# Gate and value products of the second chunk in whole float32, with the first chunks' due dates made anew

## The chip, the cores and the metric

The kernel runs on one core of one Trainium2 chip. The metric is the time of one execution on the device, in microseconds. Lower is better. A core has five engines that run side by side, each with its own queue, taken in order: TensorE (PE), which multiplies matrices; VectorE (DVE), ScalarE (ACT) and GpSimd (POOL), which work element by element; and SyncE (SP), which here issues every transfer between main memory and the core. They wait for each other by semaphores.

## The reference

The inputs are q, k and v of 8 batches, 8 heads, 576 tokens and 64 elements a head, and the weights of a channel mix of width 512 with 1024 hidden elements.

```python
k_p = k.reshape(B, H, Sp, pool, D).mean(axis=3)      # pool = 8: 72 pooled keys
v_p = v.reshape(B, H, Sp, pool, D).mean(axis=3)
scores = scale * np.matmul(q, k_p.transpose(0, 1, 3, 2))
attn = softmax(scores)                               # maximum taken off, 1e-9 added to the sum
x = np.matmul(attn, v_p)                             # heads side by side: 512 wide
x_prev = x shifted by one token, zero at a batch's start
xk = mu_k * x + (1.0 - mu_k) * x_prev
xr = mu_r * x + (1.0 - mu_r) * x_prev
k = np.maximum(xk @ w_k, 0.0)
v = k * k @ w_v
r = 1.0 / (1.0 + np.exp(-(xr @ w_r)))
out = r * v
```

## The kernel before

The 4608 tokens of all batches are one row of 13 chunks: 128, 256 and eleven times 384 tokens. A tile is 128 tokens. Each chunk goes through the same steps, and each step is a generator function that issues instructions and names what it needs:

- `softmax`, `part`, `transposed`, `transposed_rest` (one tile): scores on PE, maximum, exponential and sum on DVE and ACT, normalised on DVE or POOL, turned on PE. `BY_HEAD` lists the tiles whose exponentials are taken head by head on ACT, with the maximum as a bias and the sum taken along, in place of two passes on DVE.
- `attended` (one quarter of the width, c and g): probabilities times pooled values on PE; `shifted` and `joined` make the two mixes with the previous token, for keys (xk) and gates (xr).
- `hidden` (c, jt: 8 per chunk): the key products, xk times w_k, then the square of their positive part.
- `gate` (c, tt: one per tile): xr times w_r, and a sigmoid. `mixed` (c, tt): the squares times w_v, times the gate, and out.

**Whole and split.** A product of two float32 operands can be made in two ways here. Whole: one float32 matmul. Split: each operand x is stored as a high half h (a cast to the format float32r) and a low half l = x - h, and three float32r matmuls h*h + l*h + h*l are added. A split operand costs a cast on ACT and a subtraction on DVE or POOL: `x_parts` for the mixes (names xkh, xkl, xrh, xrl), the end of `hidden` for the squares (sh, sl), `split` for the weights (w_k, w_r, w_v from got_wk, got_wr, got_wv). Before the change, only chunk 0 is whole (`WHOLE`) and its attention and that of chunk 1 (`WHOLE_ATT`). The weights arrive as 64-bit words, and `convert` makes float32 of them (L528 on ACT, L530 and L533 on DVE). `split` (L555 on ACT, L558 on DVE or POOL by `LOW_BY`) waits until the whole products that read the full weight are done, and each split waits for the one before it, since its two halves take a buffer that the one before gave back.

**What sets the order.** The kernel builds its instruction streams before it runs: `Order.run` keeps all steps as threads, with a due date each, estimates when each engine is free, and takes the step that is ready with the earliest due date. `EARLIER` is a table that is added to the due dates by name (softmax 3, hidden 1 4, split v 2); a step that is not in it keeps its plain date. The order that comes out is fixed in the program: on the chip an engine runs its list in turn, and an instruction that waits holds up all that stand behind it. `LOADS` is the order of the first transfers on SP's queue: k, v, r and q followed by a number are keys, values, the last pooled values and queries; wk, wr and wv are the weights; c are constants. Keys and values land in staging buffers, of which few exist, so a load can wait until the sums over its predecessor are done. Two tiles under early_sl and one under early_xrl are extra landing places: they lie in the buffers that chunk 1 or 2 later use for sl and xrl. `SUM_BY` names the engine of a pooling sum (t is PE, v DVE, g POOL).

At the start PE runs `warm` (L430) and 40 fillers (L440), matmuls whose results nobody reads.

## Time and profile before

| | |
|---|---|
| runs shown | 641.62, 641.49 and 643.84 us; median 641.62 |
| profiled execution | 642.56 us, span 640.8 us |
| granted TensorE clock | 1.0 throughout |
| first matmul of chunk 0's key products | 28.91 us from the span's start |
| first matmul of chunk 2's key products | 104.58 us |
| busy over the span | PE 622.0, DVE 410.1, ACT 358.6, POOL 216.7 us |
| transfers | 50.48 MB, mean 79 GB/s |

The page gives busy time by engine, the span in slices, the transfer queues, the chain of work that ended last, the costliest groups of instructions, and the transfers. Times in the trace are from the start of the span. A line such as L1082 is a line of the kernel before. In a group of instructions, the names are out<-in with buffer numbers left out, then partitions x elements, the count, the busy time, the mean duration of one in ns, and the idle time of the engine just before them with what ended it. A whole float32 matmul is recorded as two matmuls. The records of matmuls that follow each other overlap, so the step from one to the next is read from a run of them, not from the mean of one.

### The profile page before, as it was taken

To read this page: it belongs to the slowest core of one execution; us is meant where nothing else is said; L and a number is where in the kernel's file an instruction comes from. 1 tells how busy PE (TensorE), PEld (TensorE's weight loads), DVE (VectorE), ACT (ScalarE), POOL (GpSimd) and SP (SyncE) were. 2 spreads that over 40 slices of the span, in tenths; PEclk is the share of its full clock that TensorE was granted. 3 is DMA by queue.
4 is the path that set the end of the run, shared out by engine and by line. 5 is a ranking of instruction groups with operands and counts; after the bars stand their busy time and mean duration, and the time that the engine had idled before them with its cause. 6 is when DMAs were issued, how large, how long until landed. Compare 5 with 4: busy or idle time off the path is not lost.

```text
span 640.8 us, 9433 instructions
## 1 busy us (share of the span) xinstructions
PE 622.0 (97%) x3411; PEld 552.0 (86%) x3411; DVE 410.1 (64%) x803; ACT 358.6 (56%) x788; POOL 216.7 (34%) x342
## 2 busy tenths in 40 slices
...
GB/s 338 257 389 121 92 143 46 97 136 64 109 74 50 50 1 18 173 90 34 18 27 163 58 16 34 34 25 166 58 21 38 42 17 18 34 0 17 34 1 50
DMA packets 19007, 50.48 MB, mean 79 GB/s; under 512 B 2256, under 2 KB 2512, under 8 KB 18960
## 3 DMA queue, kind: packets, MB, share of 16 engines
...
## 4 chain that ended last, share of the span: by engine, by line
PE 78%; DVE 12%; ACT 4%; POOL 3%; DMA 2%; issue 1%; SPq 0%; DVEq 0%; POOLq 0%; ACTq 0%
PE mm L1034 27%; PE mm L1115 25%; PE mm L1082 15%; PE bank L937 4%; PE sc L735 4%; DVE xm L990 2%; PE bank L839 2%; POOL xkl L1008 1%; DVE sl L1058 1%; DMA got_wk<-in_w_k 1%; POOL xrl L1008 1%; PE bank L440 1%; ACT t L950 1%; DVE pr L876 1%; DVE stage L565 1%
## 5 line engine op out<-in xcount | busy, mean ns | idle before, releaser
L1034 PE MATMUL mm<-xkh,w_k 128*128 128x384 f32 (+1 forms) x768 | 194.3, 335 | 1.1 <-DVE rk L1050 1.1
L1115 PE MATMUL mm<-w_v,sh 128*128 128x512 f32 x560 | 186.7, 396 | 0.7 <-DVE w_v L558 0.7
L1034 PEld LDWEIGHTS mm<-xkh,w_k 128*128 128x128 f32 x768 | 136.2, 188 | 3.9 <-DVE rk L1050 2.2
L1034 PE MATMUL mm<-xkl,w_k 128*128 128x384 f32 (+1 forms) x384 | 126.9, 330 | 0.0
L1115 PEld LDWEIGHTS mm<-w_v,sh 128*128 128x128 f32 x560 | 105.4, 188 | 21.6 <-DVE w_v L558 1.2
L1115 PE MATMUL mm<-w_v,sl 128*128 128x512 f32 x280 | 109.3, 390 | 0.0
L1082 PE MATMUL mm<-w_r,xrh 128*128 128x512 f32 x280 | 90.8, 396 | 1.5 <-DVE rk L1050 1.5
L990 DVE SCALAR_TENSOR_TENSOR xm<-bank,given,t 128x384 f32<-128x384 f32 (+1 forms) x96 | 54.5, 601 | 44.9 <-POOL t L965 27.2
L1056 ACT CAST sh<-rk 128x384 fp32r<-128x384 f32 (+1 forms) x96 | 48.3, 505 | 57.9 <-DVE rk L1050 57.5
L1058 DVE TENSOR_TENSOR sl<-rk,sh 128x384 fp32r<-128x384 f32 (+1 forms) x96 | 57.1, 597 | 28.0 <-ACT sh L1056 27.4
L1008 POOL TENSOR_TENSOR xkl<-xm,xkh 128x384 fp32r<-128x384 f32 (+1 forms) x48 | 48.2, 1003 | 78.2 <-ACT xkh L1006 78.0
L1034 PEld LDWEIGHTS mm<-xkl,w_k 128*128 128x128 f32 x384 | 72.2, 188 | 0.1
L950 ACT ACTIVATE t<-bank,om_sb 128x384 f32<-128x384 f32 (+1 forms) x96 | 48.0, 570 | 39.2 <-PE bank L937 39.2
L797 POOL TENSOR_TENSOR px<-e,sm 128x64 f32<-128x64 f32 (+1 forms) x33 | 10.4, 314 | 160.3 <-DVE sm L791 150.5
L1043 ACT ACTIVATE rk<-mm 128x384 f32<-128x384 f32 (+1 forms) x96 | 46.0, 480 | 33.1 <-PE mm L1034 25.9
L1082 PEld LDWEIGHTS mm<-w_r,xrh 128*128 128x128 f32 x280 | 52.6, 188 | 12.7 <-DVE rk L1050 1.9
L1125 DVE TENSOR_TENSOR rs<-mm,rs 128x512 f32<-128x512 f32 x36 | 24.6, 684 | 60.3 <-PE mm L1115 60.1
L1050 DVE SCALAR_TENSOR_TENSOR rk<-mm,rk 128x384 f32<-128x384 f32 (+1 forms) x96 | 51.6, 540 | 17.9 <-ACT rk L1043 17.7
L1115 PEld LDWEIGHTS mm<-w_v,sl 128*128 128x128 f32 x280 | 52.8, 188 | 8.9
L1082 PE MATMUL mm<-w_r,xrl 128*128 128x512 f32 x140 | 54.6, 390 | 0.0
L565 POOL TENSOR_TENSOR stage<-stage 128x512 f32<-128x512 f32 (+5 forms) x57 | 48.6, 861 | 2.0
L1008 POOL TENSOR_TENSOR xrl<-xm,xrh 128x384 fp32r<-128x384 f32 (+1 forms) x48 | 48.1, 1002 | 2.5 <-ACT xrh L1006 2.4
...
## 6 DMA issues: line engine op xcount, KB each, us to landing
...
stage<-in_vm SPq DMA_DIRECT2D x15, 512.0 KB, 4.3
got_wk<-in_w_k SPq DMA_DIRECT2D x8, 512.0 KB, 6.9
got_wv<-in_w_v SPq DMA_DIRECT2D x8, 512.0 KB, 9.6
...
got_wr<-in_w_r SPq DMA_DIRECT2D x4, 512.0 KB, 8.9
```

Source lines behind the costliest of these rows:

```text
L565: nc_eng.tensor_tensor(out=st[:, :, :w], in0=st[:, :, :w], in1=st[:, :, w:2 * w], op=ALU.add)
L735: nc.tensor.matmul(out=halves[g // 2][o:o + n, 0, k:k + 2 * KEYS], lhsT=qs[:, g, o:o + n], rhs=kbd[b % 2][:, g, :], start=True, stop=True,)
L950: nc.scalar.activation(out=ts[m][:, 1:n + 1], in_=xp, func=AF.Copy, scale=om_sb[:, m, g:g + 1])
L990: nc.vector.scalar_tensor_tensor(out=xm[:, :n], in0=bank[:, :n], scalar=mu_sb[:, m, g:g + 1], in1=ts, op0=ALU.mult, op1=ALU.add,)
L1008: nc.gpsimd.tensor_tensor(out=lo, in0=xm[:, :n], in1=hi, op=ALU.subtract)
L1034: nc.tensor.matmul(out=hp, lhsT=w[:, o], rhs=x[:, ct, :n], start=(ct == 0 and k == 0), stop=(ct == NCT - 1 and k == len(terms) - 1),)
L1043: nc.scalar.activation(out=rk[:, :n], in_=hp, func=AF.Relu)
L1050: nc.vector.scalar_tensor_tensor(out=rk[:, :n], in0=hp, scalar=0.0, in1=rk[:, :n], op0=ALU.max, op1=ALU.mult)
L1056: nc.scalar.copy(out=sh[:, :n], in_=rk[:, :n])
L1058: nc.vector.tensor_tensor(out=operand("sl", c)[:, jt, :n], in0=rk[:, :n], in1=sh[:, :n], op=ALU.subtract)
L1082: nc.tensor.matmul(out=bank, lhsT=x[:, ct, o], rhs=w, start=(ct == 0 and k == 0), stop=(ct == NCT - 1 and k == len(terms) - 1),)
L1115: nc.tensor.matmul(out=bank, lhsT=s[:, o], rhs=w, start=(jt == 0 and k == 0), stop=(jt == NJT - 1 and k == len(terms) - 1),)
```

## The change

Chunk 1's gate products and value products become whole; its key products stay split. `WHOLE_GATE` and `WHOLE_MIX` name the chunks for which that holds. With it go `x_parts` of chunk 1's gate input, the cast and the low half of its squares, and its waits for the early tiles in sl and xrl, which it no longer uses. The splits of w_r and w_v now wait for chunk 1's products too. Tile 6 joins `BY_HEAD`. The transfers at the start stand in a new order, the table of due dates is new and ends with chunk 3, where it ended with chunk 4, and the planner counts 0.43 rather than 0.86 us for a warming matmul.

```diff
--- before.py
+++ after.py
@@ -33,6 +33,8 @@
 CH = max(CHUNKS)
 
 WHOLE = (0,)
+WHOLE_GATE = (0, 1)
+WHOLE_MIX = (0, 1)
 WHOLE_ATT = (0, 1)
 TWICE = 3
 PACKED = (0, 1)
@@ -43,76 +45,66 @@
 REBASE = 2.0 ** -((1023 - 127) // 8)
 
 LOADS = (
-    "k0 k1 k2 q0 r0 q1 c0 wk0 v0 k3 q2 wk1 wk2 wk3 wk4 v1 wk5 r1 q4 wk6 wk7 q3 v3 wr0 wr1 wr2 wr3 "
-    "wv0 wv1 wv2 q5 wv3 wv4 wv5 wv6 wv7 v2 "
+    "k0 c0 wk0 q0 k1 wk1 r0 wk2 q1 q2 v0 v1 k2 wk3 q4 wk4 r1 wk5 q3 k3 wk6 v3 wk7 q5 wr0 wr1 wr2 wr3 "
+    "wv0 wv1 wv2 v2 wv3 wv4 wv5 wv6 wv7 "
 )
 
 SUM_BY = {"k0": "t", "k1": "v", "v0": "t", "v1": "t", "r0": "t", "k2": "v", "k3": "v", "v2": "g", "v3": "v", "r1": "g"}
 
-NORM_BY = {0: 'g', 1: 'v', 2: 'v', 3: 'v', 4: 'g', 6: 'g', 5: 'v'}
+NORM_BY = {0: 'g', 1: 'v', 2: 'v', 3: 'v', 4: 'g', 6: 'g', 5: 'v', 7: 'g'}
 WARMING = 4
 FILLERS = 40
 
 LOW_BY = {"k": "gvgvvvgv", "r": "gvgv", "v": "gvvggvgv"}
-BY_HEAD = ((0, 1), (2, 0))
+BY_HEAD = ((0, 1), (2, 0), (6, 0))
 
 BESIDE = (1,)
 SQUARED_ON_ACT = (8, 0)
 COPIES_ON_ACT = ()
 
 EARLIER = {
-    "warm": 192.0, "constants": 417.1, "complements": 5357.6, "loads": 265.4, "keys 0 0": 155.5,
...
+    "filling": 484.5, "warm": 561.9, "constants": 6.9, "complements": 129.2, "loads": 322.9,
...
 }
 PLAN = ""
 SPARE = 0.5
@@ -313,7 +305,8 @@
         if c in WHOLE:
             return whole_operands[kind]
         if (kind, c) not in operands:
-            dtype = F32 if kind == "pth" and c in WHOLE_ATT else F32R
+            whole = {"pth": WHOLE_ATT, "xrh": WHOLE_GATE, "sh": WHOLE_MIX}.get(kind, ())
+            dtype = F32 if c in whole else F32R
             operands[kind, c] = sb.tile(shapes[kind], dtype, name=f"{kind}_{c}", tag=kind)
         return operands[kind, c]
 
@@ -327,7 +320,8 @@
         return every(kind, c - 1) if c > 1 else []
 
     def free_of_early(c, tag):
-        return [("early", t, i) for t, n in EARLY for i in range(n) if t == tag and c not in WHOLE]
+        kept = c in {"sl": WHOLE_MIX, "xrl": WHOLE_GATE}[tag]
+        return [("early", t, i) for t, n in EARLY for i in range(n) if t == tag and not kept]
 
     slots("rs", CH // P, [P, DM])
     slots("t", 2, [P, 2, CH + 1])
@@ -426,7 +420,7 @@
         nc.vector.memset(zeros, 0.0)
         bank = yield take("bank")
         for _ in range(WARMING):
-            yield "pe", 0.86, False
+            yield "pe", 0.43, False
             nc.tensor.matmul(out=bank[:, :256], lhsT=zeros[:, :P], rhs=zeros[:, :256], start=True, stop=True)
         order.give("bank", bank)
         order.give("tmp", zeros)
@@ -980,9 +974,10 @@
         n = CHUNKS[c]
         whole = c in WHOLE
         bank, t = held["t", c, g]
-        if whole:
+        direct = whole or m and c in WHOLE_GATE
+        if direct:
             xm = operand(f"x{'kr'[m]}h", c)[:, g]
-            ts = xm[:, :n]
+            ts = xm[:, :n] if whole else t[:, m, :n]
         else:
             xm = yield take("xm")
             ts = t[:, m, :n]
@@ -994,7 +989,7 @@
             if t is not None:
                 order.give("t", t)
             order.give("mm" if whole and g == NPAIR - 1 else "bank", bank)
-        if whole:
+        if direct:
             order.make(("x", c, g, m))
         else:
             order.add(att_due[c] + g, x_parts(c, g, m, xm))
@@ -1038,7 +1033,8 @@
         order.make(("hid", c, jt))
         yield need(*before("mixed", c), *free_of_early(c, "sl"))
         sh = operand("sh", c)[:, jt]
-        rk = sh if whole else (yield take("rk"))
+        kept = c in WHOLE_MIX
+        rk = sh if kept else (yield take("rk"))
         yield act(n)
         nc.scalar.activation(out=rk[:, :n], in_=hp, func=AF.Relu)
         if c < 2 and jt < SQUARED_ON_ACT[c]:
@@ -1051,7 +1047,7 @@
                 out=rk[:, :n], in0=hp, scalar=0.0, in1=rk[:, :n], op0=ALU.max, op1=ALU.mult
             )
             order.give("mm", bank)
-        if not whole:
+        if not kept:
             yield act(n)
             nc.scalar.copy(out=sh[:, :n], in_=rk[:, :n])
             yield dve(n)
@@ -1062,7 +1058,7 @@
         order.make(("s", c, jt))
 
     def gate(c, tt):
-        whole = c in WHOLE
+        whole = c in WHOLE_GATE
         last = tt == CHUNKS[c] // P - 1
         yield need(*([("gating", c, tt - 1)] if tt else every("hid", c)))
         bank = yield take("mm")
@@ -1084,7 +1080,7 @@
                     start=(ct == 0 and k == 0), stop=(ct == NCT - 1 and k == len(terms) - 1),
                 )
         order.make(("gated", c, tt))
-        if last and whole:
+        if last and c in WHOLE:
             order.give("stage", stage[1])
         yield act(DM, "sigmoid")
         nc.scalar.activation(out=rs, in_=bank, func=AF.Sigmoid)
@@ -1093,7 +1089,7 @@
         order.make(("gate", c, tt))
 
     def mixed(c, tt):
-        whole = c in WHOLE
+        whole = c in WHOLE_MIX
         last = tt == CHUNKS[c] // P - 1
         yield need(*every("gated", c))
         if tt:
@@ -1103,7 +1099,7 @@
         for jt in range(NJT):
             yield need(("s", c, jt), ("full" if whole else "parts", "v", jt))
             yield pe(DM, whole, 1 if whole else 3)
-            if jt == 0 and whole or jt == NJT - 1:
+            if jt == 0 and c in WHOLE or jt == NJT - 1:
                 order.make(("mixing", c, tt))
             if whole:
                 terms = [(operand("sh", c)[:, jt], full["v", jt])]
@@ -1117,7 +1113,7 @@
                     start=(jt == 0 and k == 0), stop=(jt == NJT - 1 and k == len(terms) - 1),
                 )
         order.make(("mixed", c, tt))
-        if last and whole:
+        if last and c in WHOLE:
             order.give("stage", stage[2])
         yield need(("gate", c, tt))
         rs = held.pop(("rs", c, tt))
@@ -1149,7 +1145,8 @@
             at = {"k": FIRST + 2.6 * i - 4, "r": FIRST + 20 + 2 * i - 3, "v": FIRST + 28 + 2.5 * i}[kind]
             order.add(at, convert(kind, i))
             used = [("hid", c, i) for c in WHOLE] if kind == "k" else [
-                k for c in WHOLE for k in every({"r": "gated", "v": "mixed"}[kind], c)
+                k for c in {"r": WHOLE_GATE, "v": WHOLE_MIX}[kind]
+                for k in every({"r": "gated", "v": "mixed"}[kind], c)
             ]
             at = {"k": 2.1 * i - 4, "r": 15 + i, "v": 25 + 0.8 * i}[kind]
             order.add(later + at, split(kind, i, *used))
```

Three places show how the change moves instructions. Lines of the changed kernel stand 3 to 6 lower in number than those of the kernel before: L1078 is the gate's matmul (L1082), L1111 the value products' (L1115), L1029 the key products' (L1034).

The first is PE in the middle of the second chunk: the end of its key products and the start of its gates. Before:

```order
L1034 MATMUL mm_117<-xkh_440,w_k_661 128x256 x2
L1034 MATMUL mm_117<-xkl_441,w_k_661 128x256
L894 MATMUL bank_114<-ident,pr_94 128x128
L1082 MATMUL mm_119<-w_r_700,xrh_458 128x512
L1082 MATMUL mm_119<-w_r_700,xrl_459 128x512
L1082 MATMUL mm_119<-w_r_700,xrh_458 128x512
L1082 MATMUL mm_118<-w_r_700,xrh_458 128x512
L1082 MATMUL mm_118<-w_r_700,xrl_459 128x512
L1082 MATMUL mm_118<-w_r_700,xrh_458 128x512
```

Now:

```order
L1029 MATMUL mm_117<-xkh_421,w_k_674 128x256 x2
L1029 MATMUL mm_117<-xkl_422,w_k_674 128x256
L1078 MATMUL mm_119<-got_wr_588,stage_107 128x512
L1078 MATMUL mm_118<-got_wr_571,xrh_420 128x512
L1078 MATMUL mm_118<-got_wr_577,xrh_420 128x512
L888 MATMUL bank_114<-ident,pr_95 128x128
L1078 MATMUL mm_118<-got_wr_588,xrh_420 128x512
L1078 MATMUL mm_117<-got_wr_571,xrh_420 128x512
L1078 MATMUL mm_117<-got_wr_577,xrh_420 128x512
L1078 MATMUL mm_117<-got_wr_588,xrh_420 128x512
```

The three matmuls on halves (w_r with xrh, xrl, xrh) have become one on the full weight, got_wr, and chunk 0's gate (stage_107 is its input) is made in between, where it stood ahead of them.

The second is SP's queue, from the last but one of the key weights on. Before:

```order
L487 DMA got_wk_354<-in_w_k 128x1024
L487 DMA got_wk_364<-in_w_k 128x1024
L479 DMA qs_104<-in_qT 128x512
L511 DMA stage_106<-in_vm 128x1024
L487 DMA got_wr_401<-in_w_r 128x1024
L487 DMA got_wr_409<-in_w_r 128x1024
L487 DMA got_wr_419<-in_w_r 128x1024
L487 DMA got_wr_424<-in_w_r 128x1024
L487 DMA got_wv_433<-in_w_v 128x1024
L487 DMA got_wv_442<-in_w_v 128x1024
L487 DMA got_wv_454<-in_w_v 128x1024
L479 DMA qs_105<-in_qT 128x512
```

Now:

```order
L505 DMA stage_106<-in_kT 128x1152
L481 DMA got_wk_381<-in_w_k 128x1024
L505 DMA stage_106<-in_vm 128x1024
L481 DMA got_wk_552<-in_w_k 128x1024
L473 DMA qs_105<-in_qT 128x512
L481 DMA got_wr_571<-in_w_r 128x1024
L481 DMA got_wr_577<-in_w_r 128x1024
L481 DMA got_wr_588<-in_w_r 128x1024
L481 DMA got_wr_597<-in_w_r 128x1024
L481 DMA got_wv_607<-in_w_v 128x1024
L481 DMA got_wv_617<-in_w_v 128x1024
L481 DMA got_wv_625<-in_w_v 128x1024
```

The buffer stage_106 takes one load after the other. Before, only v3 (stage_106<-in_vm) stands between the last key weight and the gate weights. Now k3 (in_kT) goes into it ahead of the key weight before the last, v3 into the same buffer behind that, and the last key weight and all gate and value weights stand behind v3.

The third is DVE while the gate weights are converted and the squares of chunk 1 are made. Before:

```order
L802 TENSOR_TENSOR pm_90<-e_89,sm_99 128x512
L533 SCALAR_TENSOR_TENSOR got_wv_511<-got_wv_511,tmp_101 128x512
L1058 TENSOR_TENSOR sl_634<-rk_87,sh_583 128x256
L558 TENSOR_TENSOR w_r_737<-got_wr_409,w_r_737 128x512
L530 TENSOR_SCALAR tmp_102<-tmp_102 128x512
L874 CAST pr_95<-px_93 128x2x32
L533 SCALAR_TENSOR_TENSOR got_wv_495<-got_wv_495,tmp_102 128x512
L876 TENSOR_TENSOR pr_95<-px_93,pr_95 128x2x32
L1058 TENSOR_TENSOR sl_634<-rk_86,sh_583 128x256
L874 CAST pr_94<-px_92 128x2x32
L1050 SCALAR_TENSOR_TENSOR rk_87<-mm_117,rk_87 128x256
```

Now:

```order
L1046 SCALAR_TENSOR_TENSOR sh_531<-mm_117,sh_531 128x256
L1046 SCALAR_TENSOR_TENSOR sh_531<-mm_119,sh_531 128x256
L524 TENSOR_SCALAR tmp_101<-tmp_101 128x512
L524 TENSOR_SCALAR tmp_102<-tmp_102 128x512
L527 SCALAR_TENSOR_TENSOR got_wr_571<-got_wr_571,tmp_101 128x512
L527 SCALAR_TENSOR_TENSOR got_wr_577<-got_wr_577,tmp_102 128x512
L552 TENSOR_TENSOR w_k_674<-got_wk_552,w_k_674 128x512
L1046 SCALAR_TENSOR_TENSOR sh_531<-mm_118,sh_531 128x256
L524 TENSOR_SCALAR tmp_101<-tmp_101 128x512
L846 TENSOR_TENSOR ptl_688<-bank_115,pth_687 128x4x128
L527 SCALAR_TENSOR_TENSOR got_wr_588<-got_wr_588,tmp_101 128x512
```

The squares (L1050 before, L1046 now) are written straight to sh, and the low halves (sl) and the split of w_r have gone from between them; a split of w_k stands there instead.

92 rows, old and new, of the table EARLIER are left out of this document.

## The prediction

> **What bounds the kernel now.** I read the page's busy shares first, then the stretches between the places where the work changes, then the chain of waits inside the stretch that is not full.
>
> ```profile
> PE 622.0 (97%) x3411; PEld 552.0 (86%) x3411; DVE 410.1 (64%) x803; ACT 358.6 (56%) x788; POOL 216.7 (34%) x342
> 27.60:50.00 22.40, 18.20 (x145) 16.41 (x144) 21.29 (x45) 18.59 (x55) 14.61 (x27) 1.00 0.96 360
> 50.00:70.00 20.00, 18.25 (x88) 11.71 (x87) 19.94 (x43) 15.82 (x31) 5.98 (x6) 1.00 0.33 100
> 70.00:95.80 25.80, 21.89 (x124) 17.51 (x123) 24.50 (x48) 18.46 (x41) 8.85 (x13) 1.00 0.38 121
> 95.80:104.60 8.80, 8.73 (x51) 7.34 (x49) 8.16 (x17) 5.69 (x12) 7.91 (x15) 1.00 0.20 61
> 104.60:161.50 56.90, 54.98 (x303) 48.54 (x302) 42.03 (x82) 36.18 (x76) 27.14 (x40) 1.00 0.27 88
> 161.50:636.90 475.40, 474.38 (x2527) 426.26 (x2525) 272.58 (x511) 248.07 (x524) 147.79 (x233) 1.00 0.15 49
> ```
>
> Behind each stretch stand its length and the busy time of PE, PEld, DVE, ACT and POOL, then clock, DMA share and GB/s. From 161.5 us on, PE is busy for 474.38 of 475.40 us: nothing is to be had there but by taking PE work away. The stretch from 27.6 (the first key input of chunk 0 is being joined) to 104.6 us (the first key product of chunk 2) is another thing: PE is busy 18.20 + 18.25 + 21.89 + 8.73 = 67.1 of 77.0 us, so it stands idle for 9.9, and DVE is full. That stretch is where the second chunk lives, and where all of the change falls.
>
> ```profile
> 27.60:104.60 77.00, 73.90 (x150) 1.00 0.51 178
> 41.56 2.82 DVE got_wr L533 x2
> 66.58 0.60 DVE w_r L558
> 69.45 1.42 DVE sl L1058
> 89.78 1.58 DVE w_v L558
> ```
>
> The first row is DVE alone in that stretch: 73.90 of 77.00 us in 150 instructions, 0.49 us each. The others are pieces of the chain of waits: from 32 to 94 us it runs almost only through DVE, and among its pieces are the two kinds that the change takes out of this stretch, the low halves of chunk 1's squares (L1058) and the low halves of the gate and value weights (L558). L1058 and the last L558 are far longer there than such a piece usually is.
>
> **The change, part by part.** PE first. Chunk 1 has 2 gate tiles of 4 products and 2 value tiles of 8: 24 products of 512 columns, today three matmuls each.
>
> ```profile
> 52.39 3.71 PE mm L1082 x8
> 372.36 8.20 PE mm L1082 x36
> ```
>
> The first row is chunk 0's gate, 4 whole float32 products (each is recorded as two): 0.927 us a product. The other is 36 split matmuls of a later chunk's gate in steady state: 0.228 us each, 0.684 a product; value products have the same shape. The new PE work is 24 x (0.927 - 0.684) = +5.85 us. It is on the engine that sets the end, so it costs its full size unless it fills idle time.
>
> DVE, POOL and ACT next, by form:
>
> ```profile
> L1058 DVE TENSOR_TENSOR sl<-rk,sh 128x256 fp32r<-128x256 f32 x8 | 4.4, 551 | 0.0
> L558 DVE TENSOR_TENSOR w_r<-got_wr,w_r 128x512 fp32r<-128x512 f32 x2 | 1.4, 678 | 0.0
> L558 DVE TENSOR_TENSOR w_v<-got_wv,w_v 128x512 fp32r<-128x512 f32 x4 | 3.6, 905 | 0.4 <-ACT w_v L555 0.4
> L558 POOL TENSOR_TENSOR w_v<-got_wv,w_v 128x512 fp32r<-128x512 f32 x4 | 5.4, 1355 | 12.1 <-ACT w_v L555 12.1
> L558 POOL TENSOR_TENSOR w_r<-got_wr,w_r 128x512 fp32r<-128x512 f32 x2 | 2.8, 1405 | 9.0 <-ACT w_r L555 9.0
> L1008 POOL TENSOR_TENSOR xrl<-xm,xrh 128x256 fp32r<-128x256 f32 x4 | 3.3, 814 | 0.9 <-ACT xrh L1006 0.9
> L555 ACT CAST w_v<-got_wv 128x512 fp32r<-128x512 f32 x8 | 4.9, 615 | 2.0 <-DVE w_v L558 1.9
> L768 ACT ACTIVATE e<-sc,mx 128x72 f32<-128x72 f32 x12 | 3.7, 327 | 3.7 <-DVE e L776 3.5 <-DVE mx L762 0.2
> L776 DVE TENSOR_TENSOR e<-sc,mx 128x576 f32<-128x576 f32 x33 | 24.9, 753 | 1.3
> L735 PE MATMUL sc<-kbd,qs 128*128 128x144 f32 x248 | 36.0, 288 | 1.1 <-DMA qs<-in_qT 0.5 <-DVE e L776 0.5
> L839 PE MATMUL bank<-ident,pm 128*128 128x128 f32 x144 | 21.8, 274 | 0.5 <-DVE pr L874 0.2 <-POOL pm L802 0.2
> ```
>
> Gone for good are the 8 low squares (DVE 4.4 us), their 8 casts and 4 more on ACT, and 4 low halves of the gate input on POOL (3.3). The 12 gate and value weights are still split, but only after chunk 1's products have read them: 5.0 us of DVE and 8.2 of POOL move behind 104.6. By the order of the changed kernel, 9 tiles have been scored at that point instead of 11, so two softmaxes, each three DVE passes of about 0.75 us, move too: 4.5 us. DVE before chunk 2's first key product thus falls from 73.9 to about 73.9 - 4.4 - 5.0 - 4.5 = 60.0 us. PE there has 67.1 + 5.85, less two scorings (36.0 us for 31 of them, 8 records each, so 2.3), plus two groups of transposes that are done earlier (21.8 us for 36, so 1.2): 71.9. So PE takes over from DVE as the bound of this stretch. If no idle time were left, the whole would be worth -9.9 + 5.85 = -4.05 us; what moves behind 104.6 on PE cancels out of that.
>
> How much idle stays? DVE has 12 us of room, but the order interleaves the two closely: going along PE's order with the durations above and DVE's at 0.49 each, wk6, wk7, wr0, wr2 and wv3 come from DVE within some 2.5 us of PE's turn, on either side of it. Some of DVE's room is also eaten by POOL:
>
> ```profile
> 68.17 1.29 DVE L876 TENSOR_TENSOR pr<-px,pr 128x64 fp32r<-128x64 f32 x1
> 69.38 1.50 DVE L1058 TENSOR_TENSOR sl<-rk,sh 128x256 fp32r<-128x256 f32 x1
> 67.92 1.46 POOL L558 TENSOR_TENSOR w_r<-got_wr,w_r 128x512 fp32r<-128x512 f32 x1 [6.23 <-ACT w_r L555]
> 69.34 2.12 POOL L565 TENSOR_TENSOR stage<-stage 128x512 f32<-128x512 f32 x2
> 75.42 0.41 DVE L1058 TENSOR_TENSOR sl<-rk,sh 128x256 fp32r<-128x256 f32 x1
> ```
>
> The same L1058 takes 0.41 us alone and 1.50 beside a POOL addition, and the L876 ends just after POOL's L558. 11.5 us of such POOL work (8.2 + 3.3) leave the stretch. The Trainium skill, SBUF — State Buffer, section "Who interferes with whom", states an exclusive lock: the later of the two engines stands until the other's whole instruction is done. The rows agree. Were all of the 11.5 us such stops, as that rule has it at its strongest, DVE would be at 48.5 us rather than 60.0, would be ahead of PE at each of those places, and no idle would be left: 2.0 us less than the sum below.
>
> I leave 2.0 us of idle (bounds 0 and 8, the latter nearly all of today's).
>
> The start. Chunk 0's attention needs v1 and the softmax of its tile.
>
> ```profile
> 18.28 0.33 SPq L511 DMA_DIRECT2D stage<-in_vm  x1
> 23.05 1.95 PE L576 MATMUL mm<-stage,ident 128*128 128x128 f32 x16
> 26.00 0.39 PE L937 MATMUL bank<-whole_pth,vbd_w 128*128 128x128 f32 x2
> 8.08 1.72 PE L440 MATMUL bank<-ident 128*128 128x128 f32 x14
> ```
>
> Today v1 is issued at 18.28, when a staging buffer comes free, is summed at 23.05, and attention starts at 26.00. Now v1 goes into a tile of its own and waits for no compute. Against that, 7 fillers (the last row, 1.7 us) stand ahead of the first key sum, and weights wk0 to wk2 ahead of q1. DVE's work ahead of the first join is nearly the same as before. So the start can move by -3 (all of v1's wait) to +1.7 us (the fillers); I take -1.0, nearer the middle, since the softmaxes are still to be done. Tile 6's exponentials by head are 8 of 0.33 us on ACT (L768) in place of one pass, so 2 us more, and one DVE pass and one sum less. ACT was busy 58.6 of 77.0 us there and loses 24 casts from the stretch, so I cost it at nothing; without that room it would be 2.
>
> Behind 104.6, the 12 splits wait for chunk 1's gates and values and run one after another, an ACT cast of 0.62 and then 0.7 on DVE or 1.4 on POOL: some 20 us. Chunk 2's key products and gates cover them: 132 of a chunk's 204 split matmuls, so well over half of the 56.9 us to 161.5; its value products come last, with several us to spare. In 104.6 to 161.5 DVE has 14.9 us free and gets 9.5. I put 0.5 on this, between 0 and 5. Tables for chunk 4 have gone, so its tiles are no longer held back; PE is idle 1.0 us in all after 161.5, and I cost that at nothing, with 1 at most.
>
> Sum: -9.9 + 2.0 + 5.85 - 1.0 + 0.5 = -2.55. PE's busy time also holds about 2 us of ends of groups that overlapped no next matmul (the matmuls of the stretch from 28.9 us on, at the steps of steady state, add up to 63.7 us, its length less that to 12.0); with fewer stops, half of it goes: -1.0. Together -3.5 us. On the profiled execution, span 640.8 and 642.56 with what lies around it, that is 637.3 and 639.1; on the median of the runs shown, 641.6, it is 638.1.
>
> **The rivals.** *A bigger gain*: idle gone (-9.9 - 2.0 + 5.85 = -6.05) and a start that is 1 us earlier or a little more: -7, 634.6. For it speaks that DVE has 12 us of room, against it that each new order of this kind meets stops that nobody planned, like the 2.82 us of two L533.
>
> *PE's new work eats what DVE gives*: 6 us of idle stay (stops in DVE's and ACT's queues in other places), or the start slips by the fillers: -9.9 + 6 + 5.85 - 1 = +1, or -0.5 with half of the ends; 641.5. For it: 5.85 us are certain, the saving is not.
>
> *Slower: the weights come too late.*
>
> ```profile
> 28.84 0.33 SPq L511 DMA_DIRECT2D stage<-in_vm  x1
> 29.20 2.80 SPq L487 DMA_DIRECT2D got_wr<-in_w_r  x4
> 37.04 5.47 SPq L487 DMA_DIRECT2D got_wv<-in_w_v  x5
> 35.00:40.00 5.00, 4.84 (x43) 4.34 (x44) 4.92 (x10) 4.83 (x17) 4.75 (x7) 1.00 1.02 412
> stage<-in_vm SPq DMA_DIRECT2D x15, 512.0 KB, 4.3
> 78.03 0.50 PE L1082 MATMUL mm<-w_r,xrh 128*128 128x512 f32 x1 [1.46 <-DVE rk L1050]
> ```
>
> SP issues in order. Today v3 leaves at 28.84, the gate weights right behind it, and the last of the value weights by 42.5, on queues that move 412 GB/s. In the changed order, v3 waits for the buffer of k3, whose sums on DVE stand 33 instructions behind the first join: at 0.49 each, 27 + 16 = 43 us. wk7, q5, wr0 to wr3 and wv0 to wv2 are all behind it. v2 waits in the same way for v3's low half, 71 instructions behind the join, so until about 62; wv3 to wv7 are behind that. wv3 then lands at 62 + 4.3 + 1.3 = 67.6 and is converted by about 69.3. PE's turn for it, if PE never stops, is some 41 us after 28, so 69. There is no slack. From the point at which DVE is some 2 us later there, each further microsecond is one on PE: were DVE's instructions at 0.6, v3 would leave at 47 and v2 at 70, and PE would wait 8 us: -3.5 + 8 = +4.5, 646. Against it: the same DVE delay would hold PE up in any case, and DVE's load is lighter. The Trainium skill, TensorE: Matmul & The Clock Gate, section "Part 1: The HAM clock gate", has PE fall back to half clock after an idle window of about 3.4 us; PE's longest stop in today's stretch is the 1.46 us of the last row, so no run here shows it; with that rule this rival would be about 1.7 us longer.
>
> That the change does not do what it says (the parts still made, the casts still there) is excluded by the order: the instructions are gone.
>
> **How the numbers follow.** Forecast, -5 to -1.5: 0.42. Bigger gain: 0.20. No gain: 0.20. Late weights: 0.18. Half a per cent, 3.2 us, is about what a measurement here can tell from nothing. Below 638.4 lie the bigger gain and 0.26 of the forecast: faster 0.46. Above 644.8 lies most of the late weights: slower 0.15. The same: 0.39. Eight in ten: 634.5 to 645.0, from the bigger gain to about the middle of the last rival; the forecast's own range is 636.6 to 640.1.
>
> **What would show it.** Chunk 1's 24 whole products at 0.92 to 0.94 us. The first key product of chunk 2 at about 98 to 101 us rather than 104.6. DVE below 85% busy from the first join to there, PE idle there below 4 us, no L558 of a gate or value weight before chunk 1's gates. The chain through PE, not DVE, from about 50 us on. wv3 landed by 68. The forecast is wrong if PE waits for got_wr or got_wv conversions for more than 4 us together, if the first key product of chunk 0 is later than 30 us, or if chunk 2's gate or value products wait for L558.

## The result and the profile after

The changed kernel takes 633.1 us (632.8 to 634.2) where the kernel before takes 641.6 beside it: the ratio is 0.9862, with a 95% interval of 0.9838 to 0.9886, so 7.3 to 10.4 us are gone, and the profiled execution has a span of 630.9 us for 640.8. (The profiled execution of the kernel before took 642.56 us, 0.9 above its median, that of the changed kernel 632.79; so the two profiles lie 9.8 us apart, 1.3 more than the medians.) The forecast was 638.1 (634.5 to 645.0). The sign was right, the size was not, and the time lies below the range.

First the page's busy line of the changed kernel, then both kernels cut at the same places of the program: the first key product of chunk 0, 2, 3 and 5, and the end of PE's work. (Behind each stretch: length, busy time of PE, PEld, DVE, ACT and POOL with counts, clock, DMA share, GB/s.) The changed kernel:

```profile
PE 621.1 (98%) x3387; PEld 547.5 (87%) x3387; DVE 396.8 (63%) x794; ACT 351.9 (56%) x787; POOL 211.7 (34%) x338
...
28.06:97.78 69.72, 65.63 (x357) 45.85 (x356) 60.23 (x130) 50.43 (x130) 28.11 (x51) 1.00 0.49 174
97.78:150.07 52.29, 52.29 (x291) 46.62 (x289) 44.52 (x89) 35.55 (x78) 30.81 (x37) 1.00 0.36 123
150.07:247.89 97.82, 97.82 (x533) 88.58 (x531) 57.16 (x115) 50.98 (x105) 30.30 (x55) 1.00 0.18 60
247.89:627.00 379.11, 379.04 (x2018) 341.44 (x2016) 213.81 (x402) 198.22 (x418) 116.91 (x180) 1.00 0.14 48
```

The kernel before:

```profile
28.91:104.58 75.67, 65.74 (x389) 51.70 (x388) 72.57 (x146) 57.25 (x131) 36.46 (x53) 1.00 0.51 176
104.58:157.96 53.38, 51.86 (x287) 45.71 (x285) 39.35 (x75) 33.90 (x71) 24.83 (x36) 1.00 0.26 84
157.96:260.44 102.48, 101.05 (x551) 90.08 (x550) 67.69 (x132) 59.90 (x132) 42.06 (x69) 1.00 0.17 57
260.44:636.90 376.46, 376.46 (x1997) 339.03 (x1995) 207.60 (x387) 190.45 (x398) 108.06 (x169) 1.00 0.14 48
```

The stretch from which I had expected the gain, chunk 0 to chunk 2, is 5.95 us shorter, and DVE in it fell from 72.6 to 60.2 us. Counted from the first join, as I had forecast it, DVE fell by 12.7 us, from 73.9 to 61.2, for 13.9 and 60.0. What I had put at half a microsecond more lies in the rows behind: 53.38 became 52.29 and 102.48 became 97.82, and PE, which had 1.5 + 1.4 us of recorded idle time there, now has none.

Recorded idle time is not all that a stop costs. To see the rest I took, for each kind of matmul, the usual step from its start to the next start (the median over both kernels; a mean without stops for scores, transposes and the attention products of one kind, whose steps alternate), added the steps up as work, and called what is left of a stretch its stops. (Another choice of the usual step moves single entries by up to some 1.3 us, the changes in stops by 0.2.) By that reckoning:

| stretch (first key product to first key product) | before: length = work + stops | after | change in stops |
|---|---|---|---|
| chunk 0 to 2 | 75.67 = 59.78 + 15.89 | 69.72 = 63.18 + 6.55 | -9.34 |
| chunk 2 to 3 | 53.38 = 50.44 + 2.94 | 52.29 = 50.94 + 1.34 | -1.60 |
| chunk 3 to 5 | 102.48 = 97.88 + 4.60 | 97.82 = 96.08 + 1.73 | -2.87 |
| chunk 5 to PE's last start | 376.08 = 371.93 + 4.15 | 378.78 = 374.08 + 4.70 | +0.55 |
| sum | 607.6 = 580.0 + 27.6 | 598.6 = 584.3 + 14.3 | -13.3 |

Work rises by 4.25 us, stops fall by 13.3, and chunk 0 starts 0.84 us sooner: 4.25 - 13.26 - 0.84 = -9.85, which is how much sooner PE's last product begins.

PE's waits in the first stretch, of the changed kernel (engine, line, waited for: us in total, times, longest):

```profile
PE bank L833 <- POOL pm L796: 2.4, 1, 2.4
PE mm L1078 <- DVE got_wr L527: 0.8, 1, 0.8
PE mm L1029 <- DVE sh L1046: 0.5, 1, 0.5
...
```

One stop is left that matters, ahead of tile 7's transposes. The pieces of the chain of waits that lead to it (start, length, what):

```profile
61.71 7.99 DMA got_wv<-in_w_v
...
76.30 2.53 ACT e L762 x16
79.67 1.04 POOL pm L796
...
91.68 1.25 POOL stage L559
...
94.92 1.01 POOL pm L796
95.97 0.66 PE bank L833 x4
96.63 1.72 PE mm L1111 x4
```

From about 62 to 96 us the chain goes through the weights' arrival, ACT, POOL and some pieces of DVE; I had expected it to go through PE from 50 us on. Behind chunk 2's start the view of PE's waits is empty in the changed kernel up to 310 us. In the kernel before it holds, from 104.6 to 310 us:

```profile
PE bank L894 <- DVE pr L876: 1.5, 2, 1.1
PE bank L894 <- ACT e L782: 0.4, 1, 0.4
PE mm L1034 <- DVE rk L1050: 0.4, 1, 0.4
...
```

### The profile page after: what moved, and what is told of

The parts are those of the page before. It is cut to its first block, busy times and chain, and to the rows that moved or that the text cites. A ratio compares the mean times of both kernels' runs of the same rounds, so it can differ in the third digit from the quotient of the medians.

```text
span 630.9 us, 9355 instructions
## 1 busy us (share of the span) xinstructions
PE 621.1 (98%) x3387; PEld 547.5 (87%) x3387; DVE 396.8 (63%) x794; ACT 351.9 (56%) x787; POOL 211.7 (34%) x338
## 4 chain that ended last, share of the span: by engine, by line
PE 78%; DVE 8%; ACT 4%; POOL 4%; DMA 3%; issue 2%; SPq 0%; POOLq 0%; DVEq 0%; ACTq 0%
PE mm L1029 26%; PE mm L1111 26%; PE mm L1078 13%; PE bank L931 4%; PE sc L729 4%; PE bank L833 2%; DMA got_wr<-in_w_r 1%; DMA got_wv<-in_w_v 1%; POOL xkl L1003 1%; ACT e L762 1%; DVE xm L985 1%; POOL pm L796 1%; PE bank L424 1%; DVE mx L753 1%; DVE kbd L601 1%
## 5 line engine op out<-in xcount | busy, mean ns | idle before, releaser
L1029 PE MATMUL mm<-xkh,w_k 128*128 128x384 f32 (+1 forms) x768 | 193.4, 334 | 0.5 <-DVE sh L1046 0.5
L1111 PE MATMUL mm<-w_v,sh 128*128 128x512 f32 x528 | 174.2, 395 | 0.0
L1029 PEld LDWEIGHTS mm<-xkh,w_k 128*128 128x128 f32 x768 | 136.1, 188 | 2.7 <-issue 1.1
L1029 PE MATMUL mm<-xkl,w_k 128*128 128x384 f32 (+1 forms) x384 | 126.7, 330 | 0.0
L1111 PEld LDWEIGHTS mm<-w_v,sh 128*128 128x128 f32 x528 | 99.2, 188 | 19.8 <-issue 0.2
L1111 PE MATMUL mm<-w_v,sl 128*128 128x512 f32 x264 | 103.0, 390 | 0.0
L1078 PE MATMUL mm<-w_r,xrh 128*128 128x512 f32 x264 | 85.7, 396 | 0.0
L985 DVE SCALAR_TENSOR_TENSOR xm<-bank,given,t 128x384 f32<-128x384 f32 (+1 forms) x92 | 52.5, 606 | 43.2 <-POOL t L959 29.2
L1052 ACT CAST sh<-rk 128x384 fp32r<-128x384 f32 x88 | 45.1, 514 | 52.4 <-DVE rk L1046 52.0
L1029 PEld LDWEIGHTS mm<-xkl,w_k 128*128 128x128 f32 x384 | 72.2, 188 | 0.0
L1054 DVE TENSOR_TENSOR sl<-rk,sh 128x384 fp32r<-128x384 f32 x88 | 50.4, 573 | 24.6 <-ACT sh L1052 24.0
L1046 DVE SCALAR_TENSOR_TENSOR rk<-mm,rk 128x384 f32<-128x384 f32 x88 | 48.6, 553 | 18.9 <-ACT rk L1039 18.6
L1078 PEld LDWEIGHTS mm<-w_r,xrh 128*128 128x128 f32 x264 | 49.6, 188 | 10.4 <-ACT rs L1086 0.4
L1039 ACT ACTIVATE rk<-mm 128x384 f32<-128x384 f32 x88 | 43.1, 490 | 27.6 <-PE mm L1029 25.5
L1111 PEld LDWEIGHTS mm<-w_v,sl 128*128 128x128 f32 x264 | 49.7, 188 | 8.5
L559 POOL TENSOR_TENSOR stage<-stage 128x512 f32<-128x512 f32 (+5 forms) x57 | 47.9, 848 | 15.8 <-PE bank L833 13.1
L1078 PE MATMUL mm<-w_r,xrl 128*128 128x512 f32 x132 | 51.4, 390 | 0.0
L1003 POOL TENSOR_TENSOR xrl<-xm,xrh 128x384 fp32r<-128x384 f32 x44 | 44.9, 1020 | 2.3 <-ACT xrh L1001 2.2
```

What stands on the lines that cost most here:

```text
L559: nc_eng.tensor_tensor(out=st[:, :, :w], in0=st[:, :, :w], in1=st[:, :, w:2 * w], op=ALU.add)
L985: nc.vector.scalar_tensor_tensor(out=xm[:, :n], in0=bank[:, :n], scalar=mu_sb[:, m, g:g + 1], in1=ts, op0=ALU.mult, op1=ALU.add,)
L1003: nc.gpsimd.tensor_tensor(out=lo, in0=xm[:, :n], in1=hi, op=ALU.subtract)
L1029: nc.tensor.matmul(out=hp, lhsT=w[:, o], rhs=x[:, ct, :n], start=(ct == 0 and k == 0), stop=(ct == NCT - 1 and k == len(terms) - 1),)
L1039: nc.scalar.activation(out=rk[:, :n], in_=hp, func=AF.Relu)
L1046: nc.vector.scalar_tensor_tensor(out=rk[:, :n], in0=hp, scalar=0.0, in1=rk[:, :n], op0=ALU.max, op1=ALU.mult)
```

## The experiments

In all of them but one the order is not made by the planner but written out: `PLAN` holds the names of the steps in the order that it took in the changed kernel (or in the kernel before), and `Order.run` goes by that list, so that an edit moves nothing else. Where an order was put onto a kernel for which it was not made, the first step of the list that is ready is taken. Because the list stands in the file, lines of these kernels are some 318 higher than in the kernel that they come from (L1429 is L1111, L1151 is L833). Beside them the kernel before took 641.96 to 642.01 us.

### Is PE the bound of the first stretch? Five whole products less, and five more

```diff
-            for k, (x, w) in enumerate(terms):
+            for k, (x, w) in enumerate(terms if (c, tt, ct) != (1, 0, 1) else ()):
...
-            for k, (s, w) in enumerate(terms):
+            for k, (s, w) in enumerate(terms if c != 1 or jt not in (2, 4) else ()):
```

> The changed kernel in exactly its own order, with 5 of the second chunk's 24 whole products left out (one of the gate's, four of the values'; so the output of that chunk lacks them). In the changed kernel's trace a whole product steps on by 2 x 0.429 = 0.858 us, so 5 are 4.29 us, about what all 24 cost above split ones (24 x (0.858 - 0.682) = 4.2). Theory A (PE sets the pace in that stretch and the whole products cost their full size): 633.1 - 4.3 = 628.8 us, between 628.3 and 630. Rival B (the stretch is still set by DVE or by the weights' arrival, and the whole products fill time in which PE would stand idle): no less than 631.5 us, with longer stops of PE ahead of got_wv or of chunk 2's inputs.

Measured: 634.37 us, ratio 0.9884 (0.9870 to 0.9898). Not 4.3 us less than the changed kernel, but 1 more or the same. PE's timeline of this kernel around the stop, and the clock in four stretches (length, busy times in the order of the fences above, clock):

```profile
91.17 1.02 PE L1429 MATMUL mm<-got_wv,stage 128*128 128x512 f32 x2
95.82 0.66 PE L1151 MATMUL bank<-ident,pm 128*128 128x128 f32 x4 [3.63 <-POOL pm L1114]
```

```profile
93.38:96.80 3.42, 0.98 (x6) 0.75 (x7) 2.60 (x6) 1.91 (x5) 2.73 (x8) 1.00 0.00 0
96.80:100.20 3.40, 3.40 (x7) 1.84 (x6) 1.56 (x5) 0.29 (x1) 2.42 (x3) 0.50 0.71 210
```

PE came to tile 7's transposes sooner and waited 3.63 us instead of 2.38, until the same moment (95.8 us); and after so long a stop its clock was halved for one stretch of 3.4 us, which cost half of that, 1.7 us. Rival B's time holds (no less than 631.5 us); the longer stop is at tile 7's transposes, a place that it had not named.

```diff
+            if c == 1 and jt in (2, 4) or (c, tt, jt) == (1, 0, 6):
+                terms = terms * 2
             for k, (s, w) in enumerate(terms):
```

> The changed kernel in exactly its own order, with 5 of the second chunk's 16 whole value products made twice (into the same sum, so that the output counts them twice). PE gets 5 x 0.858 = 4.3 us of work more between 66 and 92 us. Leaving 5 out had gained nothing. Theory W (PE waits there for the others): the stop of 2.4 us at 93 to 96 us takes up part of it, so 633.1 + 1 to 2.7 = 634 to 636 us. Theory P (PE sets the pace): 633.1 + 3.8 to 4.5 = 637 to 637.6 us.

Measured: 634.72 us, ratio 0.9883 (0.9865 to 0.9901). The stop is now

```profile
PE bank L1151 <- POOL pm L1114: 0.3, 1, 0.3
```

so 2.1 of the 4.3 us went into it, and the profiled stretch from chunk 0 to chunk 2 grew by 2.3. Theory W's number holds: in the changed kernel about two microseconds of the whole products before chunk 2 cost nothing.

### Is it DVE? More and less work for it, in the same order

```diff
-        kept = c in {"sl": WHOLE_MIX, "xrl": WHOLE_GATE}[tag]
+        kept = c in WHOLE
...
+        if kept and c == 1:
+            unread = operand("sl", c)[:, jt, :n]
+            nc.vector.tensor_tensor(out=unread, in0=rk[:, :n], in1=rk[:, :n], op=ALU.subtract)
         order.make(("s", c, jt))
```

> The changed kernel in exactly its own order, with 8 more subtractions on DVE, one behind each square of the second chunk (128x256, where the kernel before made the low halves of the squares; nobody reads them here). They add 8 x about 0.4 to 0.55 = 3.2 to 4.4 us of DVE work between about 40 and 56 us. Theory A (the relief of DVE is a main part of the gain, since DVE is busy 20.6 of 22 us from 28 to 50 us and two stops of PE there, 0.5 and 0.8 us, are on DVE already): 633.1 + 2 to 4 = 635 to 637 us, with longer stops of PE ahead of got_wr and of chunk 1's later key products. Rival B (the gain comes from the order, DVE has slack): within 0.7 us of 633.1.

The first edit has the second chunk wait for the early tiles in sl and xrl again, since sl is written again. Measured: 635.35 us, ratio 0.9891 (0.9876 to 0.9906), 2.2 us above the changed kernel; the intervals of the two ratios overlap, but all five executions (634.5 to 638.2) lie above all four of the changed kernel (632.8 to 634.2). The eight instructions, by form, and a wait that grew:

```profile
L1378 DVE TENSOR_TENSOR sl<-sh 128x256 fp32r<-128x256 f32 x8 | 4.6, 580 | 0.3
```

```profile
PE mm L1347 <- DVE sh L1364: 1.9, 2, 1.0
```

The wait for the squares went from 0.5 to 1.9 us, and one for ACT in front of a key product (L1357) from 0.2 to 1.5. The execution profiled here is the slowest of the five (638.2 us), so its stretch to chunk 2 grew by 3.5 us, more than the 2.2 of the medians. By the medians, 4.6 us of DVE work at this place is worth about half of its size, as theory A had it. The opposite edit took the maximum and the sum of tiles 3 to 8 over 8 keys a head instead of 72:

```diff
-            nc.vector.tensor_reduce(out=mx[:, o], in_=sv, axis=AX.X, op=ALU.max)
+            few = slice(0, 8 if 3 <= i <= 8 else KEYS)
+            nc.vector.tensor_reduce(out=mx[:, o], in_=sv[:, :, :, few], axis=AX.X, op=ALU.max)
...
-            nc.vector.tensor_reduce(out=sm[:, mine], in_=e[:, mine], axis=AX.X, op=ALU.add)
+            nc.vector.tensor_reduce(out=sm[:, mine], in_=e[:, mine, :, few], axis=AX.X, op=ALU.add)
```

> The changed kernel in exactly its own order, but the maximum and the sum of tiles 3 to 8 go over the first 8 keys of each head instead of 72 (so their softmax is wrong). That takes 12 x about 0.65 = 7.8 us of work off DVE between 33 and 116 us and nothing off PE. Theory W (up to about 116 us the elementwise engines, DVE first, set the pace and PE's whole products fill time in which it would wait): PE's stops there, 7 us in the changed kernel, shrink by 3 to 6: 627.5 to 630.5 us. Theory P (PE sets the pace there by now, as the prediction had it): not below 631.5 us.

Measured: 633.02 us, ratio 0.9854 (0.9836 to 0.9872), the same as the changed kernel. By form, between 33 and 117 us:

```profile
L1072 DVE TENSOR_REDUCE mx<-sc 128x8 f32<-128x64 f32 x6 | 1.3, 213 | 0.0
L1097 DVE TENSOR_REDUCE sm<-e 128x8 f32<-128x64 f32 x5 | 1.1, 218 | 3.1 <-ACT e L1095 2.9
```

An instruction took 0.21 us rather than 0.75, and DVE's busy time from 28 to 97.8 us fell from 60.3 to 54.2, for nothing: PE waited 2.1 us at the same place, for the same POOL instruction. Theory W fell here. The time fits theory P's bound, but P had fallen with the five products left out, which gained nothing either. So neither PE's work nor the softmax work of DVE sets the length of this stretch by itself. What is left is the chain through ACT and POOL shown above; that the stop at its end hangs on POOL's sums is shown below, for the rest of the chain it is argued from the trace.

### The last stop, at 96 us

Three edits went at it: tile 7 normalised on DVE; batch 2's value sums (the 2.6 us of L559) behind tile 7's normalisation; and these sums there together with tile 7's exponentials by head.

```diff
-NORM_BY = {0: 'g', 1: 'v', 2: 'v', 3: 'v', 4: 'g', 6: 'g', 5: 'v', 7: 'g'}
+NORM_BY = {0: 'g', 1: 'v', 2: 'v', 3: 'v', 4: 'g', 6: 'g', 5: 'v', 7: 'v'}
```

> The changed kernel in its own order, with tile 7 normalised on DVE rather than POOL. In the changed kernel PE's longest stop is 2.38 us up to 95.97 us, until POOL's normalisation of that tile, which stands behind 2.62 us of pooling additions on POOL; DVE idles 0.78 us there. Theory A (the stop is POOL's queue): PE goes on about 1.3 us sooner, 631.8 us, between 631 and 632.3. Rival B (the tile's exponentials or DVE's chain end last, or DVE hands the delay on to chunk 2's inputs): 632.8 to 634 us.

Measured: 633.23 us, ratio 0.9864 (0.9849 to 0.9880). The stop stayed at 2.4 us, now for DVE: its normalisation stands behind a joined input that waits for POOL's copies, and these stand behind the same sums. For the second edit, the three steps on POOL of "values 2 0" (and with them its two later ones, on ACT and DVE) stand behind the two on POOL of "softmax 7" in the list, one step to a line here:

```diff
 PLAN = (
...
-values 2 0
...
-values 2 0
...
-values 2 0
...
 softmax 7
...
 softmax 7
+values 2 0
+values 2 0
+values 2 0
...
 )
```

> The changed kernel, in its own order but for one step: the pooling sums of batch 2's values (2.6 us on POOL from 91.6 us, not needed before chunk 3) stand behind tile 7's normalisation on POOL instead of ahead of chunk 2's last mix and of that normalisation. In the changed kernel PE stops for 2.4 us up to 95.97 us for that normalisation, and the chain of waits comes from these sums. Theory A (POOL's block sets that stop; with the normalisation on DVE it stayed, since DVE then waited for POOL's copies behind the same block): the stop shrinks by 1 to 2.4 us and the first key product of chunk 2 comes at 69.7 - 1 to 2.4 us after that of chunk 0; 631 to 632.2 us. Rival B (tile 7's maximum, exponential and sum on DVE and ACT, which end at 93.3 us, are as late): not below 632.5 us.

Measured: 633.58 us, ratio 0.9875 (0.9859 to 0.9891). The first key product of chunk 2 came 67.8 us after that of chunk 0 instead of 69.7, as theory A had it, and the gain was gone by chunk 3: 55.1 us from chunk 2 to 3 instead of 52.3, with a new wait

```profile
PE bank L1206 <- DVE pr L1188: 1.4, 1, 1.4
```

The third edit also adds tile 7 to `BY_HEAD`:

```diff
-BY_HEAD = ((0, 1), (2, 0), (6, 0))
+BY_HEAD = ((0, 1), (2, 0), (6, 0), (7, 0))
```

> The changed kernel with tile 7's exponentials by head on ACT too (DVE 1.5 us less, ACT some 2 us more), and the pooling sums of batch 2's values behind that tile's normalisation on POOL, the order otherwise its own. Theory W (DVE and POOL set the stop at 96 us, and the moved sums alone gained 2 us there but lost it again at DVE's next result): 631 to 632.5 us. Rival (ACT, busy 16 of 21 us there, is as late): 633 to 636 us.

Measured: 636.21 us, ratio 0.9909 (0.9892 to 0.9927), 3 us slower than the changed kernel: ACT was late, as the rival had it, with one wait of 3.2 us ahead of the next tile's scores, and behind it the clock was at 0.5 for 3.4 us, which cost up to 1.7 of the 3.

```profile
PE sc L1046 <- ACT e L1079: 3.2, 1, 3.2
```

None of the three beats the changed kernel: each time another result came last, on DVE twice and on ACT once.

### The whole products without the new order

The kernel before, with the change's code for whole gate and value products in chunk 1 but with its own loads, dates and order of steps (the steps no longer made are taken out). In a first run the 12 splits of gate and value weights came in a block, each as soon as chunk 1's products had read its weight, the first already among chunk 1's value products.

```diff
+WHOLE_GATE = (0, 1)
+WHOLE_MIX = (0, 1)
...
-PLAN = ""
+PLAN = (
...
+)
...
-                name = self.plan.pop(0)
-                at, t = next((at, t) for at, t in ready if t[6] == name)
+                can = {t[6]: (at, t) for at, t in ready}
+                at, t = can[self.plan.pop(next(k for k, name in enumerate(self.plan) if name in can))]
```

> The kernel before with the whole gate and value products of its second chunk alone: its own order of steps, loads and dates, only that the steps of the parts no longer made are gone (4 casts and low halves of the gate input, 8 of the squares) and the 12 splits of w_r and w_v come as soon as chunk 1 is through. PE gets 24 x (0.858 - 0.682) = 4.2 us of work more, DVE 4.4 us less, and 5.0 more of DVE's move behind chunk 1. Theory W (the whole products carry the gain, since they take work off DVE, which sets the pace): DVE's 9.4 us less are worth 6 to 9 us of PE's stops, less 4.2: 641.6 - 2 to 5 = 637 to 640 us. Theory O (the new order and loads carry it): the stops that stay in the old order leave 641 to 645 us.

Measured: 653.09 us, ratio 1.0173 (1.0158 to 1.0189). Both theories missed, since one stop of chunk 2's key products, and a clock that was at 0.5 for 10.2 us around it, cost more than all the rest:

```profile
117.26 1.01 PE L1354 MATMUL mm<-xkh,w_k 128*128 128x384 f32 x2 [8.58 <-DVE rs L1446]
```

The stretch from chunk 0 to 2 took 76.2 us here, no less than before; the splits began in it, and it too had a clock at 0.5 for 3.4 us.

In a second run each split stands in the list after as many of chunk 2's products as in the changed kernel.

> The kernel before with whole gate and value products in its second chunk, in its own order, as in the run that came to 653 us; but the 12 splits of w_r and w_v no longer stand in one block behind chunk 1: each stands among chunk 2's products where the changed kernel has it. In the earlier run the stretch from chunk 0's to chunk 2's first key product took 76.2 us (75.7 before: 4.25 us more work, 3.7 us less of stops), and 10 us were lost behind it, at one stop of 8.6 us ahead of a key product of chunk 2 and in a halved clock after it. Theory B (the block of splits made that stop): it goes, and what is left is what the whole products are worth in the old order, +0.6 us and a little for the splits: 642 to 644.5 us. Rival C (chunk 2 cannot take in 12 splits without such a stop in the old order): 648 us or more.

Measured: 647.49 us, ratio 1.0085 (1.0057 to 1.0113); the 8.6 us stop is gone, the kernel is still 5.5 us slower than before, and neither B nor C had that. The stretch from chunk 0 to 2 took 72.3 us (work 64.0, stops 8.3): **3.4 us less than in the profile before, with the whole products alone**. (Two kernels below that have the order of the kernel before up to chunk 2 unchanged took 74.7 us there, so the gain is 2.4 to 3.4.) All of it and more was lost from chunk 2 to 3, which took 61.3 us for 53.4. PE's waits there, and two stretches behind the longest of them:

```profile
PE bank L1212 <- DVE xm L1309: 2.2, 1, 2.2
PE sc L1053 <- DVE e L1094: 2.0, 1, 2.0
```

```profile
105.02:108.44 3.42, 0.97 (x5) 0.36 (x3) 1.14 (x2) 1.35 (x3) 2.77 (x6) 1.00 0.00 0
108.44:111.85 3.41, 3.19 (x10) 3.19 (x11) 2.40 (x3) 2.61 (x8) 3.33 (x5) 0.50 0.00 0
```

So the moved splits are not free by nature. In the old order the stretch in which they stand is 8 us longer (up to 3.4 of it from two halved stretches of the clock); in the new order they cost nothing that can be seen. That the splits alone make the 8 us is not shown.

### The new order without the whole products

First the changed kernel's own list of steps, with split products in chunk 1 and the steps for their parts put in where they can first be made:

```diff
-WHOLE_GATE = (0, 1)
-WHOLE_MIX = (0, 1)
+WHOLE_GATE = (0,)
+WHOLE_MIX = (0,)
```

> The changed kernel with split gate and value products in the second chunk: its loads, dates and order of steps, the steps of the parts put in where they can first be made (the split of a gate or value weight right behind its conversion). PE has 4.2 us of work less, DVE 9.4 us more ahead of chunk 2, POOL 11.5 and ACT some 12 more. By the 2.2 us that 3.2 to 4.4 us of subtractions on DVE cost in this order: theory W (the whole products carry the gain): 637 to 643 us, as DVE's and POOL's work stops PE for more than the 4.2 us it saves. Theory O (the order and the loads carry it): 630 to 635 us.

Measured: 669.23 us, ratio 1.0432 (1.0410 to 1.0454), far off both theories. Then the same edit of the two tables alone, with the order left to the planner:

> The changed kernel with split gate and value products in the second chunk again, its loads and dates, and the order that the kernel's own planner makes of that (where the run with a fixed order came to 669 us). Theory F (loads and dates fit whole products alone: the value weights wv3 to wv7, which leave at 60 us, can be split only after they have landed at 69 and been converted, and 8 splits one after another at about 1.4 us hold the value products until about 82, where the changed kernel begins them at 66): 645 to 660 us, with chunk 1's value products later than 80 us. Theory O (the new order is better whatever the products): 632 to 640 us.

Measured: 679.00 us, ratio 1.0574 (1.0554 to 1.0593). Theory F's mechanism holds in kind, its size was far too small: chunk 1's value products began at 115 us in the first run and at 99 in the second, where the changed kernel has them at 66. Of PE's waits in the second run, three rows:

```profile
PE bank L888 <- DVE pr L870: 9.6, 2, 5.1
PE sc L729 <- DVE e L770: 7.0, 4, 2.5
PE mm L1111 <- DVE w_v L552: 5.5, 1, 5.5
```

The new loads bring the last five value weights some 20 us later than the old ones (issued from 60.3 us on, where they left between 37.0 and 42.5). With whole products they need only be converted; with split ones the splits and what stands behind them in the queues of DVE, ACT and POOL hold PE up for tens of microseconds. The stops brought the clock down as well: up to chunk 2 it was at 0.5 for 27 us in the first run and for 51 in the second, which by half of that cost up to 14 and 26 of the 36 and 48 us by which this stretch is longer than in the changed kernel. The loads and the dates belong to the whole products.

### Where do the stops behind chunk 2's start come from?

The kernel before, unchanged in what it computes, with its own order up to a seam and the relative order of the changed kernel behind it. The seam lies at chunk 2's first key product, at its first gate product, and at chunk 3's first key product. The edit is a `PLAN` each time, and the lines that take the first step that is ready, as above.

> The kernel before, unchanged in what it computes and in its order up to chunk 2's first key product (104.58 us in its trace); from there on its steps are in the relative order that the changed kernel has. In the kernel before, PE's stops from there to 310 us, taken as the steps from one matmul to the next above the usual step, add up to about 4.1 us more than in the changed kernel, all at softmax results, squares and joined inputs on DVE. Theory A (those stops come from the old due dates of chunks 2 to 4): they go, and the time is 641.6 - 3.5 to 4.5 = 637 to 638 us, with the first key product of chunk 2 still at 104.6. Rival B (they come from DVE being late at 104.6 after the split second chunk, and the changed kernel is free of them because DVE was relieved): at least 2.5 us of stops stay, 640 to 642 us.

> The kernel before in its own order up to chunk 2's first gate product (125.6 us in its trace), and from there on in the relative order of the changed kernel. So chunk 2's key products have the inputs that they had, and the seam that cost 3.6 us and a halved clock for 6.8 us with the seam at 104 us should not come. From 125 us to 310 us the kernel before has stops of about 2.3 us above the usual step (at 160, 199, 201, 248 and 253 us). Theory A (they come from the old due dates): they go, 641.8 - 2.3 = 639.5 us, between 638.8 and 640.3. Rival B (they come from what is late by then, whatever the order): 641.3 us or more.

> The kernel before, in its own order up to chunk 3's first key product (158 us in its trace) and from there on in the relative order of the changed kernel. In the runs with this seam at 104 and 125 us, the stretch from chunk 3's to chunk 5's first key product took 97.8 us, as in the changed kernel, where the kernel before takes 102.5 (1.8 us of that is work that lies elsewhere then), but what the seam itself cost took it back. Theory A (the old order of chunks 3 and 4 costs some 2.4 us up to the end, and nothing else stands in the way): 641.9 - 2.4 = 639.5 us, between 638.8 and 640.3. Rival B (the seam takes it back here too): 641 us or more.

Measured, in this order: 643.06 us (1.0022, 1.0011 to 1.0033), 643.11 us (1.0018, 1.0003 to 1.0032) and 642.64 us (1.0008, 0.9998 to 1.0019). None gained. PE's waits at the three seams, in that order (103 to 160, 124 to 160 and 157 to 215 us):

```profile
PE mm L1353 <- POOL xkl L1327: 1.9, 1, 1.9
PE mm L1353 <- ACT xkh L1325: 1.7, 1, 1.7
```

```profile
PE bank L1213 <- DVE pr L1195: 2.7, 1, 2.7
```

```profile
PE mm L1352 <- DVE rk L1368: 1.4, 3, 0.8
PE bank L1212 <- DVE pr L1194: 0.6, 2, 0.4
```

Each seam loses about what lies behind it, as the rival B of the third run had it. But in the first two the stops further on are gone: the stretch from chunk 3 to chunk 5 takes 97.8 us, as in the changed kernel, where every kernel with the old order there takes 102.5 (before, and the two with whole products alone); and all the others with the changed kernel's written order in chunks 2 to 5 have 97.8, whatever was done to chunk 1. In the third run, whose new order begins with this stretch itself, it takes 100.7, and PE is still idle in it for 2.05 us (1.43 before). So the 2.9 us of stops from chunk 3 to 5 belong to the order of the steps, not to the whole products; an order that begins with chunk 2's gates is early enough for that, one that begins with chunk 3 is not. That they can be had without what the new order does ahead of it is not shown: no seam let them through.

## Why the prediction was wrong, by its own steps

**The first stretch: the sum was right, in part by luck.** I had idle time fall by 7.9 us and the ends of groups by 1.0, together 8.9; stops fell by 9.34. But recorded idle time fell by only 5.84 us (from 9.93 to 4.09), and the rest, 3.5 us, is overlap of the records, for which I had 1.0: two errors that cancel. Nor was "PE takes over from DVE as the bound" right: with five products less PE gained nothing.

DVE came out at 61.2 us for 60.0, and that is in part luck too. The Trainium skill's lock (SBUF — State Buffer, section "Who interferes with whom"), taken at its strongest, had 48.5 us. Some of that came: instructions that both kernels have got shorter. Before, two conversions of gate weights took 2.90 us beside subtractions on POOL that lasted from 41.34 to 43.83; now all four take 2.6.

```profile
41.48 2.90 DVE L533 SCALAR_TENSOR_TENSOR got_wr<-got_wr,tmp 128x512 int32<-128x512 int32 x2
```

```profile
L527 DVE SCALAR_TENSOR_TENSOR got_wr<-got_wr,tmp 128x512 int32<-128x512 int32 x4 | 2.6, 681 | 0.0
L870 DVE TENSOR_TENSOR pr<-px,pr 128x64 fp32r<-128x64 f32 x3 | 0.6, 213 | 0.0
```

The subtractions in the last row took 0.79 us each in this stretch before. Over all forms that both kernels have, at equal counts, DVE is 4.4 us shorter. So by an estimate 13.9 + 4.4 - 12.7 = 5.6 us of other work came into the stretch, which the forecast had not counted.

**The start: right in size.** 0.84 us for 1.0; over the profiles of eight kernels with the new start chunk 0's first key product lies at 28.1 us in the mean (27.4 to 28.7), over six with the old one at 29.2 (28.9 to 29.6).

**Late weights: the mechanism was there, the price was not.** v3 left at 41.7 us (43 estimated) and v2 at 59.8 (62):

```profile
41.72 0.33 SPq L505 DMA_DIRECT2D stage<-in_vm  x1
...
59.84 0.33 SPq L505 DMA_DIRECT2D stage<-in_vm  x1
```

```profile
66.39 3.70 PE L1111 MATMUL mm<-got_wv,sh 128*128 128x512 f32 x8
```

The last row is the first four value products of chunk 1, wv0 to wv3: that of wv3 began at about 69.0 us (66.39 + 3 x 0.86), without a wait, where I had wv3 converted by 69.3 and PE's turn for it at 69. There was indeed no slack, but nothing fell behind by the 2 us from which the rival decides. PE waited 0.8 us for a gate weight and for no value weight. Only with split products did the late loads cost (669 and 679 us).

**"24 x (0.927 - 0.684) = +5.85": mis-sized, 4.25.** A run of chunk 1's whole products in the changed kernel:

```profile
59.67 4.46 PE L1078 MATMUL mm<-got_wr,xrh 128*128 128x512 f32 x10
```

Ten records, of which the last is 0.59 us long: (4.46 - 0.59) / 9 = 0.43 us a step, 0.86 a product. I had divided a row of eight by four, and so counted once per four products the tail of the last record, which overlaps the next matmul, and the row's first step, which is 0.1 us longer than the others. The text on how to read the page says that the step is to be read from a run, and I read it from a short one. Also, not all of this work was on the path: with five products fewer nothing was gained, and of five more half was hidden in the stop at 96 us. "It costs its full size unless it fills idle time" was the right sentence, and the second half of it applied to about 2 us.

**"Behind 104.6 ... I put 0.5 on this, between 0 and 5": wrong, -3.9.** This is the step that took the time out of the range: it is off by 4.4 us, which alone makes 633.7 of 638.1, below 634.5, while the 1.6 us of the whole products alone would have left 636.5. Stops from chunk 2 to PE's end fell by 1.60 + 2.87 and rose by 0.55. I had read the shares of busy time there (54.98 of 56.90 us, 474.38 of 475.40), put what was missing down as not worth costing, and asked only whether the moved splits would add to it. Two things were wrong in that. The eight stops there, 2.9 us of recorded idle, are 4.3 us above the usual steps, since each also loses the 0.17 us by which a matmul's record overlaps the next one. And a new order of the steps of chunks 2 and 3, with plain dates behind them, could take them away as easily as add to them: it did (shown above for the 2.9 us between chunks 3 and 5; for the 1.6 between chunks 2 and 3 no run separates order from products), and it covers the splits beside, where the old order was 8 us longer with them. The bounds should have begun at -4 us, not at 0.

**The signs named.** The first key product of chunk 2 came at 97.8 us, just ahead of the 98 to 101 that I named; DVE was busy for 86% of the stretch, not under 85; the chain did not go through PE from 50 us on. The rival called a bigger gain (634.6 us, with no idle left) came nearest in time, but by another way: 4.1 us of idle stayed, and the rest of the gain came from behind the stretch. None of the three signs that I had named for a wrong forecast came; all three looked for waits or delays, none for a gain.

**What of the 8.5 us is due to what.** The profiles, 9.8 us apart, allow only a rough split. Up to chunk 2 the changed kernel is 5.0 to 5.95 us faster: two other kernels with exactly the old order up to there took 74.7 us for 75.7, though each had a halved stretch of the clock. Of this the whole products alone, in the old order, give 2.4 to 3.4 us where the splits stand behind the stretch, and no gain where they begin in it (76.2). The other 2.6 us came with the new order and loads, as did the 0.8 at the start. Behind chunk 2, the 2.9 us between chunks 3 and 5 are shown to lie in the order. Neither part works alone: 647 to 653 us for the products without the order, 669 to 679 for the order without the products. What stays open is how much of the 9.3 us of stops ahead of chunk 2 is DVE's relief and how much ACT's and POOL's: giving DVE 4.6 us back costs 2.2, taking another 6 away gains nothing.
